# Zero pads and constants filled by VectorE or by ScalarE, and a new order of all operations, in a gated linear attention followed by an MLP mixer

## The chip, the cores and the metric

The kernel runs on one core of a Trainium2 chip. Five engines take part: TensorE (PE; matmuls, with weight loads as a queue of their own), VectorE (DVE), ScalarE (ACT), GpSimd (POOL) and SyncE (SP). Each works through its own list of instructions in order; semaphores tie them together. The metric is the device time of one execution in microseconds (us). Before the change three runs took 174.65, 175.15 and 175.16 us; the median is 175.15.

## The reference

The first half is a gated linear attention over 4 batches, 8 heads, 768 steps and 48 features. Its result, seen as x with 384 features, goes through a mixer: two matmuls over the steps, then two over the features, each pair with a relu between and a residual sum behind.

```python
f = 1.0 / (1.0 + np.exp(-f_logit))
for t in range(S):
    state = f[:, :, t, :, None] * state + np.einsum('bhd,bhe->bhde', k[:, :, t], v[:, :, t])
    y[:, :, t] = np.einsum('bhd,bhde->bhe', q[:, :, t], state)

xt = x.transpose(0, 2, 1)
h = np.maximum(xt @ w_tok1, 0.0) @ w_tok2
u = x + h.transpose(0, 2, 1)
h2 = np.maximum(u @ w_ch1, 0.0) @ w_ch2
return u + h2
```

## The kernel before

Each batch is cut into 6 chunks of 128 steps. For a chunk, ScalarE makes the logarithm of the gate from f (`exp`, then `ln`, lines 366 and 367, or 383 and 387 in batch 0). A low part (`lo`) holds what a bf16 cut of the logarithm leaves out, so that TensorE can add the logarithms up in bf16 with a triangular matrix (`sums`). ScalarE turns the sums into factors `G` and `Gi`, VectorE multiplies q and k by them (`gated`), TensorE transposes both (`turn`), a copy brings them back to SBUF (`turned`), TensorE makes the scores, VectorE masks them (`masked`), and TensorE makes the output of the chunk from the masked scores (`within`, or part of `y`) and from the state of the chunks before (`y`). The state itself goes through `parts` (k times v on TensorE), `tsum` and `state` on VectorE, and `spread`, two copies into a block-diagonal tile `state_bd`. In batch 0 two chunks are handled as a pair (`gates_pair` and `pair`, lines 376 and 590), with other lines for the same steps: sums are L607 and L610, turns L636, parts L657, scores L668, masks L698.

The mixer of a batch follows: `tok1` (L750), a relu into `h1T`, `tok2` (L766), the residual sum `u`, a turn (`ut`, L804, or a transposing DMA), `ch1` (L819) with a relu into `zT` (L352 on ScalarE, L354 on VectorE), `ch2` (L838), the last sum (L844) and the store. The mixer of one batch is interleaved with the attention of the next, so that TensorE has the long matmuls of the one between the short ones of the other.

Nothing of this order is found while the kernel runs. Every operation is recorded in a plan with a number, the engines that may do it and the PSUM bank that it uses. The string `ORDER` (line 34) lists all numbers in the order in which they are issued; a letter behind a number picks the engine (A for ScalarE, D for VectorE, G for POOL, else the first of its list), figures behind colons pick the PSUM banks. An entry `z15` puts 15 filler matmuls of 512 columns (L870) into TensorE's list; they read a tile of ones, `steady`, and write a bank that nobody reads. Since engines work in order, an operation early in the list can hold up everything behind it on its engine.

The loads of q, k, v, of the weights and of f from batch 1 on are issued by POOL (L264 and L270), and their bytes go through one queue. The three loads of f for batch 0 and the stores are issued by SP.

Ahead of all that stand the constants, one operation each (`memset` and `once`, lines 273 to 324): the triangular matrix `tri`, identity and masks, and fills. Heads are 48 wide but laid out in 64 columns, so the columns 48 to 63 of the logarithm `L`, of its low part `Llo` and of the gated `qh` and `kh` are zeroed once; `state_bd` is zeroed, and the last 32 rows of `grow` are filled with ones. All the fills are memsets on VectorE:

```python
    for m in PAIRS:
        memset(f"L{m}p", L[0][:, 2 * m:2 * m + 2, :, D:64], 0.0, [("L", 0, 2 * m), ("L", 0, 2 * m + 1)], 200)
```

## Time and profile before

| | before |
|---|---|
| median of three runs | 175.15 us (174.65 to 175.16) |
| profiled execution | 174.64 us |
| its span, first to last instruction | 172.7 us |
| granted TensorE clock | 1.000 |
| TensorE busy | 164.5 us, 95% |
| VectorE busy | 124.8 us, 72% |
| ScalarE busy | 111.2 us, 64% |
| POOL busy | 81.9 us, 47% |

The profile comes from one execution. Some 1.9 us of it lie outside the span. A share of busy time is a mean over the whole span; TensorE's matmuls overlap and their ends are modelled, so its 95% does not say that it works at its peak. The chain of work that ended last, which is followed back from the last instruction, tells which engine set the end at each moment. In a row of a group stand the line, engine, operation, shapes and count, then the busy time and the mean duration of one in nanoseconds, then the idle time ahead of it and what ended it. A row of the chain or the timeline begins with the start and the duration in microseconds. A row of the stretches gives the limits, the length, then the busy time (and count) of TensorE, its weight loads, VectorE, ScalarE and POOL, the granted clock, the DMA share and GB/s.

### The profile page before, as it was taken

The page shows a single profiled execution, that of the slowest core. Times are in us where ns is not written, and L with a number is a line of the kernel's source. Part 1 is how long each engine was busy: PE and PEld are TensorE (multiplying, and loading weights), DVE is VectorE, ACT ScalarE, POOL GpSimd, SP SyncE. Part 2 cuts the span into 40 slices and gives each one's busy share as a digit, 9 for nine tenths or more (in the row PEclk, how much of TensorE's full clock was granted, in tenths as well). Part 3 has the DMA queues.
Part 4 walks back from the last instruction along what each step waited for, and adds up shares of the span by engine and source line. Part 5 has one row for each costly group of instructions (what it writes and reads, how often), then busy time and mean ns, then how long its engine had stood idle before and what let it go on. Part 6 is the DMA issues. An engine that isn't in the chain of part 4 may idle for free.

```text
span 172.7 us, 4466 instructions
## 1 busy us (share of the span) xinstructions
PE 164.5 (95%) x1764; PEld 103.6 (60%) x1764; DVE 124.8 (72%) x278; ACT 111.2 (64%) x251; POOL 81.9 (47%) x106
## 2 busy tenths in 40 slices
PE   6989899999999999999999999999999999999991
PEld 2457545566676765676667566656665656566660
DVE  5999868798989686989989787777857365433042
ACT  3989596999795637999999755189971410362200
POOL 2999904999636959999759613110001040000000
PEclk9999999999999999999999999999999999999999
DMA  5999999999994899999999954678430036800026
GB/s 149 217 173 181 244 198 209 159 121 111 198 136 26 203 161 127 222 95 91 145 68 112 142 24 91 148 206 197 126 61 6 0 68 211 311 5 0 0 96 229
DMA packets 89573, 22.74 MB, mean 132 GB/s; under 512 B 82288, under 2 KB 88736, under 8 KB 89552
## 3 DMA queue, kind: packets, MB, share of 16 engines
q0 software_dynamic: 69600, 13.77, 93.5%
q1 hardware_dynamic: 19952, 8.69, 19.0%
q8 instruction: 14, 0.23, 0.5%
q14 instruction: 7, 0.06, 0.1%
HBM read 25.17 MB, written 4.72 MB: 173 GB/s over the span
## 4 chain that ended last, share of the span: by engine, by line
PE 78%; ACT 8%; DVE 8%; DMA 2%; issue 2%; DVEq 0%; ACTq 0%
PE ps L819 26%; PE ps L838 24%; PE ps L766 4%; PE ps L750 3%; PE ps L495 3%; PE ps L408 2%; PE ps L560 2%; DMA f_sb<-in_f_logit_dram 2%; DVE AmT L536 2%; PE ps L556 2%; PE ps L870 1%; PE ps L424 1%; PE ps L636 1%; PE ps L456 1%; PE ps L668 1%
## 5 line engine op out<-in xcount | busy, mean ns | idle before, releaser
L819 PE MATMUL ps<-uT,w_ch 128*128 128x384 bf16 x288 | 52.3, 326 | 0.2
L838 PE MATMUL ps<-w_ch,zT 128*128 128x384 bf16 (+2 forms) x300 | 52.4, 320 | 0.0
L352 ACT ACTIVATE zT<-ps 128x384 bf16<-128x384 f32 x64 | 29.5, 490 | 17.3 <-PE ps L819 16.6
L838 PEld LDWEIGHTS <-zT 128*128 128x128 bf16 x300 | 28.0, 98 | 17.2
L819 PEld LDWEIGHTS <-w_ch 128*128 128x128 bf16 x288 | 27.3, 98 | 17.6 <-issue 0.3
L536 DVE TENSOR_TENSOR AmT<-ps,tri_bf 128x512 bf16<-128x512 f32 x36 | 23.4, 684 | 2.0 <-PE ps L408 1.1
L844 DVE TENSOR_TENSOR x_nat<-x_nat,ps 128x384 f32<-128x384 f32 (+2 forms) x25 | 12.8, 534 | 13.2 <-PE ps L838 12.9
L354 DVE TENSOR_SCALAR zT<-ps 128x384 bf16<-128x384 f32 x32 | 16.9, 553 | 7.5 <-PE ps L819 6.7
L348 POOL CAST state_bd<-state 48x192 bf16<-48x192 f32 x19 | 6.5, 342 | 29.8 <-DVE state L549 19.9
L264 POOL DMA_DIRECT2D qk_sb<-in_k_dram x16 | 15.8, 988 | 2.0 <-issue 2.0
L344 ACT ACTIVATE x_bf<-ps 128x384 bf16<-128x384 f32 x17 | 8.4, 492 | 13.0 <-PE ps L560 10.2
L264 POOL DMA_DIRECT2D qk_sb<-in_q_dram x16 | 15.9, 998 | 0.0
L264 POOL DMA_DIRECT2D v_sb<-in_v_dram x16 | 15.8, 989 | 0.0
L348 POOL CAST u_bf<-x_nat 128x384 bf16<-128x384 f32 x12 | 6.6, 564 | 19.2 <-DVE x_nat L782 11.5
L782 DVE TENSOR_TENSOR x_nat<-x_nat,ps 128x384 f32<-128x384 f32 x21 | 10.5, 550 | 4.6 <-PE ps L766 4.6
L750 PE MATMUL ps<-x_bf,w_tok 128*128 128x384 bf16 x48 | 13.3, 326 | 0.1
L374 POOL TENSOR_TENSOR Llo<-L 128x384 bf16<-128x384 f32 x13 | 10.8, 846 | 5.4 <-ACT L L367 5.2
L870 PE MATMUL ps<-x_nat 128*128 128x512 bf16 x32 | 10.8, 471 | 1.5 <-DVE x_nat L279 1.5
L485 DVE TENSOR_TENSOR qk<-qk_sb,GG 128x768 bf16<-128x768 bf16 x18 | 10.1, 569 | 1.0 <-ACT GG L468 0.9
L472 ACT ACTIVATE grow<-ps 32x384 f32<-32x384 f32 x15 | 7.0, 481 | 5.2 <-PE ps L457 5.0
L766 PE MATMUL ps<-h1T,w_tok 128*128 128x384 bf16 x48 | 9.4, 326 | 0.3 <-DVE h1T L354 0.3
L344 ACT ACTIVATE state_bd<-state 48x192 bf16<-48x192 f32 x21 | 7.5, 359 | 3.0 <-DVE state L549 2.3
(96 smaller groups left out, 264.3 us busy)
## 6 DMA issues: line engine op xcount, KB each, us to landing
out_dram<-x_nat SPq DMA_DIRECT2D x23, 192.0 KB, 2.1
f_sb<-in_f_logit_dram POOLq DMA_DIRECT2D x3, 1152.0 KB, 10.8
f_sb<-in_f_logit_dram SPq DMA_DIRECT2D x3, 384.0 KB, 4.1
w_ch<-in_moe_w_ch_dram POOLq DMA_DIRECT2D x2, 576.0 KB, 13.7
qk_sb<-in_q_dram POOLq DMA_DIRECT2D x12, 96.0 KB, 6.5
qk_sb<-in_k_dram POOLq DMA_DIRECT2D x12, 96.0 KB, 6.4
v_sb<-in_v_dram POOLq DMA_DIRECT2D x12, 96.0 KB, 5.0
w_ch<-in_moe_w_ch_dram POOLq DMA_DIRECT2D x1, 1152.0 KB, 10.1
```

The lines of the kernel that those rows point to most:

```text
L264: lambda eng=eng, into=into, of=of: eng.dma_start(out=into, in_=of),
L344: nc.scalar.activation(out_, in_, AF.Copy, bias=0.0, scale=1.0)
L348: nc.gpsimd.tensor_copy(out_, in_)
L352: nc.scalar.activation(out_, in_, AF.Relu, bias=0.0, scale=1.0)
L354: nc.vector.tensor_scalar(out_, in_, 0.0, None, ALU.max)
L536: add(("masked", b, c, p), DVE, lambda half=half, made=made: nc.vector.tensor_tensor(half, made(), tb4, ALU.mult), need=["tri_bf"], make=[ ...
L750: add(("tok1", b, rt, kt), PE, lambda rt=rt, kt=kt, pm=pm: nc.tensor.matmul(banks[pm.at][:, 0:DM], lhsT=w_tok1[:, kt, rt * 128:(rt + 1) * ...
L766: nc.tensor.matmul(banks[pm.at][:, 0:DM], lhsT=w_tok2[:, kt, tt * 128:(tt + 1) * 128], rhs=h1T[:, kt, :], start=(kt == 0 and not held), st ...
L819: nc.tensor.matmul(banks[pm.at][:, 0:384].rearrange("p (n t) -> p n t", t=128), lhsT=w[:, kt, c0:c0 + 128], rhs=uT[:, rows3, kt, :], start ...
L838: nc.tensor.matmul(banks[pm.at][:, 0:n1 - n0], lhsT=zT[:, kt, tt * 128:(tt + 1) * 128], rhs=w_ch2[:, kt, n0:n1], start=(kt == 0), stop=(kt ...
L844: add(("sum", b, tt, n0), DVE, lambda un=un, pm=pm, n=n1 - n0: nc.vector.tensor_tensor(un, un, banks[pm.at][:, 0:n], ALU.add), make=[("x_n ...
L870: nc.tensor.matmul(banks[NBANK - 1][0:rows, 0:cols], lhsT=steady[:, 0:rows], rhs=steady[:, 0:cols], start=True, stop=True)
```

## The change

Three things change. A new helper `fill` records the pads of `L`, `Llo`, `qh` and `kh`, the ones of `grow` and the zeros of `state_bd` as operations that either VectorE (memset) or ScalarE may do; ScalarE writes a copy of `steady`, scaled by the value.

```diff
+    def fill(name, tl, value, make, own, n):
+        op = once(name, (DVE, ACT), None, make, own)
+        def run():
+            if op.engine == DVE:
+                nc.vector.memset(tl, value)
+                return
+            p0 = 128 - tl.shape[0]
+            src, dims = steady[p0:128, 0:n], list(tl.shape[1:])
...
+            nc.scalar.activation(tl, src, AF.Copy, bias=0.0, scale=value)
+        op.fn = run
...
-        memset(f"L{m}p", L[0][:, 2 * m:2 * m + 2, :, D:64], 0.0, [("L", 0, 2 * m), ("L", 0, 2 * m + 1)], 200)
+        fill(f"L{m}p", L[0][:, 2 * m:2 * m + 2, :, D:64], 0.0, [("L", 0, 2 * m), ("L", 0, 2 * m + 1)], 200, 256)
...
-            memset(f"{n}{i}", tl[:, :, D:64], 0.0, [(n, i)], 105)
+            fill(f"{n}{i}", tl[:, :, D:64], 0.0, [(n, i)], 105, 128)
...
-        memset(f"sbd{i}", state_bd[i], 0.0, [("sbd", i)], 200)
+        fill(f"sbd{i}", state_bd[i], 0.0, [("sbd", i)], 140, 384)
```

The string `ORDER` is another one from its first entry to its last. It was made with a longer time set for the fetches of TensorE's instructions. By it, seven fills go to ScalarE. Decoded, the two lists begin so on the engines that the prediction speaks of (`1:` marks a constant, `f`, `q`, `k`, `v` are loads by batch and first chunk, other names are operations by batch and chunk):

```
TensorE before: z15, sums 0, sums 1, sums 2, sums 3, turn 0q, parts 0, turn 1q, turn 0k, turn 2q, turn 1k, sums 5, turn 3q, scores 1, turn 2k, z1, ...
TensorE after:  z14, sums 0, sums 1, z1, sums 2, sums 3, parts 0, turn 0q, turn 0k, turn 1q, turn 1k, sums 4, z2, scores 0, sums 5, turn 2q, scores 1, ...
ScalarE before: exp 0, ln 1, exp 2, ln 0, ln 2, exp 4, ln 4, G 0, Gi 0, G 1, Gi 1, ...
ScalarE after:  1:kh0, 1:L2p, 1:Llo1p, 1:qh1, 1:qh0, 1:L1p, exp 0, ln 0, ln 1, exp 2, ln 2, Gi 0, exp 4, Gi 1, G 1, G 0, ln 4, ...
POOL before:    tri, q0, k0, v0, q2, k2, w_tok1, v2, lo 5, k4, q4, f of batch 1, v4, spread 1, w_tok2, w_ch1, w_ch1, ...
POOL after:     tri, k0, q0, v0, k2, q2, v2, v4, q4, k4, w_tok1, f of batch 1, w_tok2, w_ch1, w_ch1, spread 1, ...
```

From the first loads of chunks 4 and 5 to the second token matmul of batch 0 they go on so:

```
TensorE before: ... within 0, scores 3, y 1, z1, turn 4k, turn 4q, turn 5k, turn 5q, z2, tok1, z1, tok1, tok1, z3, scores 4, tok1, within 2, z3, scores 5, y 2, y 3, z3, parts 4, tok1, within 4, y 4, ...
TensorE after:  ... within 0, z3, scores 3, z2, turn 4k, y 1, turn 5k, turn 4q, z1, turn 5q, scores 2, tok1, z3, scores 5, tok1, z1, scores 4, tok1, tok1, within 2, z3, y 2, parts 4, y 3, within 4, ...
VectorE before: ... gated 4q, gated 4k, gated 5k, gated 5q, state 2, masked 2, masked 3, tsum 3, masked 3, state 3, masked 4, masked 4, masked 5, masked 5, tsum 4, state 4, ...
VectorE after:  ... state 1, gated 4k, gated 4q, gated 5k, tsum 2, masked 3, state 2, gated 5q, tsum 3, masked 3, masked 2, state 3, masked 2, masked 5, masked 4, masked 5, masked 4, tsum 4, state 4, ...
```

The number of filler matmuls is 31 (32 before). Of the operations that may run on more than one engine, 18 relus into `zT` go from ScalarE to VectorE and 14 the other way; seven copies into `u_bf` go from POOL to ScalarE and four back; six low parts go from POOL to VectorE and two back; ten state copies go from POOL to ScalarE and twelve back. The work itself, apart from one filler, is the same.

In the changed file a line ahead of `fill` stands 1 further down and a line behind it 19.

More of the change, by code (lines that the diff above doesn't have):

```diff
@@ L75 @@
[L75 to L77 removed]
+32 33 6D 5D 34 10D 16D 12A 9A 20 15D 8A 13A 0 11A 21 1 7A 35 24 2 27 49 14D 23 36 22 29 26 3 28 50 30 37 51 52D 54 53D
+38 31 25 18D 55 z14 100:0 39 105:1 56D 102 40 58 57D 104 z1 137:2 43 107 106 110 142:3 101 17D 42 59 103 109 41
@@ L78 @@
+1035 1039 1036 1028:2 1046 1047 1040 804 1019 1041 560 1024 1051 1042 1029 1037 1052 1020 1025 1021 1030 1022 1026
+1027 1031 1032
 """
@@ L294 @@
     for m in PAIRS:
-        memset(f"L{m}p", L[0][:, 2 * m:2 * m + 2, :, D:64], 0.0, [("L", 0, 2 * m), ("L", 0, 2 * m + 1)], 200)
-        memset(f"Llo{m}p", Lall[:, 2 * m:2 * m + 2, :, D:64], 0.0, [("Llo", 2 * m), ("Llo", 2 * m + 1)], 110)
+        fill(f"L{m}p", L[0][:, 2 * m:2 * m + 2, :, D:64], 0.0, [("L", 0, 2 * m), ("L", 0, 2 * m + 1)], 200, 256)
+        fill(f"Llo{m}p", Lall[:, 2 * m:2 * m + 2, :, D:64], 0.0, [("Llo", 2 * m), ("Llo", 2 * m + 1)], 110, 256)
     alone = [(b, c) for b, c in sorted(TOTALS) if b or c // 2 not in PAIRS]
@@ L305 @@
     for i in range(NROW):
-        memset(f"grow{i}", grow[i][96:128], 1.0, [("grow", i)], 600)
+        fill(f"grow{i}", grow[i][96:128], 1.0, [("grow", i)], 560, 512)
     for i in range(len(state_bd)):
-        memset(f"sbd{i}", state_bd[i], 0.0, [("sbd", i)], 200)
+        fill(f"sbd{i}", state_bd[i], 0.0, [("sbd", i)], 140, 384)
     if PAIRS:
```

87 lines of the change are left out of this document (44 added, 43 removed).

## The prediction

> **What bounds the kernel now.** I read the shares and the chain of the page first, then the stretches of 8 us, then the chain in order of time.
>
> ```profile
> PE 164.5 (95%) x1764; PEld 103.6 (60%) x1764; DVE 124.8 (72%) x278; ACT 111.2 (64%) x251; POOL 81.9 (47%) x106
> PE 78%; ACT 8%; DVE 8%; DMA 2%; issue 2%; DVEq 0%; ACTq 0%
> ```
>
> TensorE carries the kernel: 78% of the chain. Its busy time is modelled, so what it must do is read from a stretch in which it does nothing else (from the chain in order of time):
>
> ```profile
> 145.52 11.21 PE ps L819 x69
> ```
>
> One matmul of 384 columns takes 11.21/69 = 0.1625 us here, not the 0.32 us of the groups. The change leaves out no real matmul, so only time in which TensorE stands or runs fillers (L870, a 128x512 matmul into an unused bank) can be won. Where is that? The stretches:
>
> ```profile
> 8.00:16.00 8.00, 7.17 (x150) 5.14 (x150) 7.46 (x23) 7.16 (x17) 7.96 (x9) 1.00 1.86 176
> 16.00:24.00 8.00, 6.96 (x150) 4.12 (x150) 6.14 (x15) 6.09 (x12) 5.50 (x8) 1.00 1.36 216
> 24.00:32.00 8.00, 7.45 (x149) 4.43 (x149) 5.96 (x13) 6.38 (x16) 3.70 (x7) 1.00 1.31 203
> 80.00:88.00 8.00, 7.69 (x85) 5.21 (x84) 7.37 (x17) 7.83 (x20) 4.99 (x7) 1.00 2.36 121
> ```
>
> The first figure after the length is TensorE's busy time. Between 8 and 32 us it stands for 0.83 + 1.04 + 0.55 = 2.4 us even by the generous count, and fills more with L870; later a stretch loses 0.31 us at the worst. So the head, up to the first second-stage token matmul (L766), is where a new list can win, and the chain says what it waits for there:
>
> ```profile
> 4.19 0.85 ACT f_sb L387
> 6.76 0.56 DVE Llo L396
> 10.34 0.97 DVE qk L629
> 17.62 0.71 issue
> 21.54 1.03 ACT zT L344
> 22.97 1.03 ACT zT L344
> 24.05 0.42 PE ps L668 x16
> 28.00 0.36 DVE tsum L728
> 28.91 0.36 ACT state_bd L344
> 31.41 1.62 PE ps L766 x9
> ```
>
> From 4 to 12.5 us it is gates: exponential, low part, gated q. One step there is dear, the first gated product at 0.97. From 21.5 to 24 us two copies of transposed q and k stand one after the other on ScalarE before the scores of chunks 4 and 5 (L668). From 28.00 to 31.41 runs a fixed chain (state, its copy, output, x_bf, tok1, relu) of 3.41 us.
>
> **The change, part by part.**
>
> *Fills on ScalarE.* Seven move from VectorE to ScalarE: three strided pads of 128 elements (kh0, qh1, qh0) and three of 256 (L2p, Llo1p, L1p) ahead of the first exponential, and state_bd 1 (384) later, where ScalarE has room. No row of before shows a scaled copy of ones; the nearest are ScalarE's smallest and its usual tile, and on the other side VectorE's zeroing:
>
> ```profile
> L625 ACT ACTIVATE gpair<-ps 128x8 f32<-128x8 f32 x3 | 0.6, 183 | 0.0
> L352 ACT ACTIVATE zT<-ps 128x384 bf16<-128x384 f32 x64 | 29.5, 490 | 17.3 <-PE ps L819 16.6
> L277 DVE MEMSET Llo<- 128x128 uint32 x3 | 0.5, 165 | 0.1
> L277 DVE MEMSET L<- 128x256 f32 x3 | 0.8, 272 | 0.0
> L175 ACT ACT_TABLE_LOAD x1 | 1.3, 1283 | 0.7 <-PEq L888 0.7
> L387 ACT ACTIVATE f_sb<-f_sb 128x768 f32<-128x768 f32 x3 | 2.5, 832 | 2.2 <-DMA f_sb<-in_f_logit_dram 2.2
> ```
>
> On a straight line between 183 (8 elements) and 490 ns (384), 128 elements cost 0.28 and 256 cost 0.39: six fills are 3 x 0.28 + 3 x 0.39 = 2.0 us; the ends are 6 x 0.18 = 1.1 and 6 x 0.49 = 2.9. ScalarE waits 2.17 us for the first f anyway, between its table load (0.74 + 1.28 = 2.02) and the exponential at 4.19. Taken at 2.0 the fills end at 4.0 and cost nothing; at the upper end they end at 4.96 and everything behind the exponential is 0.8 late. I take nothing, by the line. VectorE is relieved of 0.17 + 2 x 0.27 = 0.7 us and three shorter ones, of which only what stands before the low parts counts.
>
> The Trainium skill, "VectorE: DVE Perf Modes", section "Zero memsets can be issued as uint32 (trn2)", speaks against this part: a zero fill of 2-byte elements is done there at 4 bytes per element. The rows agree: Llo's 256 bf16 are 128 uint32 in 165 ns, and ScalarE has no such halving, so the same pad is my 0.39 there. By that rule the change buys some 1 us of VectorE with 2.0 us of ScalarE, a bad trade wherever ScalarE is the later of the two; here the wait for f pays for it.
>
> *First sums.* The list puts logarithm 0 right behind the first exponential and the low parts 0, 1 behind it. VectorE's queue decides: tri at 3.6 us, then ten small constants. Before, eleven such took 3.85 to 5.65, 1.8 us; so the low part of chunk 0 starts near 5.85 (6.76 before), that of chunk 1 ends at 6.95. TensorE's first sums were at 7.12 behind 15 fillers; with 14 they start at 6.9. Gain 0.2.
>
> *No pair of low parts at the same time.* Before, the last one ran on POOL beside VectorE's:
>
> ```profile
> 9.36 1.06 DVE L396 TENSOR_TENSOR Llo<-L 128x384 bf16<-128x384 f32 x1
> 9.97 1.12 POOL L396 TENSOR_TENSOR Llo<-L 128x384 bf16<-128x384 f32 x1
> ```
>
> 1.06 beside POOL, 0.56 alone (6.76 in the chain). The new list has both on VectorE, later, behind the first four gated products: 0.5 us, and the 0.97 product is back at 0.35. What is late next is a load: POOL's queue moves bytes one load behind the other, and its landings are
>
> ```profile
> L264 POOL DMA_DIRECT2D v_sb<-in_v_dram x1: 881/881/881, 5.7 to 5.7; - x1
> DMA to landing us min/median/max: 5.6/5.6/5.6
> L264 POOL DMA_DIRECT2D f_sb<-in_f_logit_dram x1: 2250/2250/2250, 12.8 to 12.8; - x1
> DMA to landing us min/median/max: 11.9/11.9/11.9
> L270 POOL DMA_DIRECT2D w_ch<-in_moe_w_ch_dram x1: 760/760/760, 17.4 to 17.4; - x1
> DMA to landing us min/median/max: 12.6/12.6/12.6
> f_sb<-in_f_logit_dram POOLq DMA_DIRECT2D x3, 1152.0 KB, 10.8
> qk_sb<-in_q_dram POOLq DMA_DIRECT2D x3, 192.0 KB, 5.8
> ```
>
> The first v lands at 5.7 + 5.6 = 11.3, and at 11.4 after, since one more long fill stands ahead of tri. In the new list the parts of pair 0, which need v, stand ahead of its turns, so the turns wait too. Their prices:
>
> ```profile
> 14.68 0.22 PE ps L636 x4
> 14.90 0.35 PE ps L668 x16
> 17.14 0.37 PE ps L657 x32
> ```
>
> Parts from 11.45 to 11.85, four turns to 12.7; the copy of q (ScalarE, 1.03) runs from 12.6 and that of k (VectorE, 0.69) from 12.8, side by side, and the first scores start near 13.8, where before they start at 14.9.
>
> *Chunks 4 and 5.* All nine q, k, v loads of batch 0 now stand ahead of w_tok1. From the first v (11.3) to f of batch 1 (12.8 + 11.9 = 24.7) the queue moved five loads of 192 KB, w_tok1 with 384 and f with 1152: 2496 KB in 13.4 us, 1.03 us for a load. So the last k, six loads behind v, lands at 17.6, and I take 18.6, a load later; w_tok1 two load times on, at 20.6 at the latest. VectorE is through with the masks of pair 0 (four at 0.62 from 14.6, gated products between) at 17.4 and with state 1 at 17.7, so gated products of pair 2 run from 18.7. TensorE: scores 3 to 19.0, two fillers to 19.4, turn 4k, y 1 (its state copy on ScalarE ends at 19.6, behind glast), turn 5k to 20.05; the k copy runs from 20.1 to 21.1. The last q turn waits for gated 5q, which stands behind tsum 2, a mask and state 2 on VectorE and ends at 21.05; the q copy runs from 21.5 to 22.5: scores from 22.55, against 24.05. Five masks then stand on VectorE, at 2.48/4 = 0.62 each:
>
> ```profile
> 15.29 2.48 DVE L698 TENSOR_TENSOR zT<-ps,x_nat 128x512 bf16<-128x512 f32 x4
> ```
>
> Starting at 22.75, behind a state, they end at 25.9, and the chain tsum to L766 of 3.41 us, which is the same operations in both lists, starts at 25.9 instead of 28.0. Gain at this point 2.1 us; the 0.2 of the first sums is in it.
>
> *What I charge against it.* My steps carry no unexplained wait, and before has one, the 0.71 "issue" in the middle of scores at 17.62: TensorE waits for nothing that the profile shows. As many small matmuls stand there in the new list, so I charge 0.7: 1.4 us. The Trainium skill, "Runtime: NRT & Kernel Launch", section "Instruction fetch mechanics", says instructions come in blocks of 256 and that a crossing is mostly hidden; by it I would charge nothing and say 2.1. The trace shows the stall, so the charge stands.
>
> *Behind the head.* Some 95 relus, copies and subtractions change between ScalarE, VectorE and POOL, but the totals hold: 18 relus go to VectorE and 14 come back, and the list has 256 operations for ScalarE (250 before), 276 for VectorE (277) and 97 for POOL (102). What the list does lose is distance: between the turn of chunk 1 of batch 1 and its scores stand one L819 group of three, the parts and one scores, 0.49 + 0.37 + 0.27 = 1.1 us (the small ones from the chain's rows below), where before two groups, a sums and the same parts and scores stood, 1.95.
>
> ```profile
> 44.34 0.36 PE ps L424 x16
> 44.70 0.55 PE ps L408 x16
> L346 DVE COPY qkT<-ps 128x1024 bf16<-128x1024 bf16 x9 | 6.1, 688 | 1.0 <-PE ps L495 1.0
> ```
>
> The copy needs 0.69 and about 0.2 around it, so 0.2 is left instead of 1.0. Going through both lists in this way, I count 12 reads behind the head with under 0.3 us to spare, against 5. One missed costs at most the 0.31 of the worst stretch; I charge two thirds of one, 0.2.
>
> Sum: 2.1 - 0.7 - 0.2 = 1.2 us. The profiled execution took 174.64 with a span of 172.7, so 173.4 and a span near 171.5. The median of the runs, 175.15, lies 0.5 above that execution; from it the sum gives 173.95. I say 173.7, between the two. No change can be told within 0.3%, 0.5 us: 174.6 to 175.7.
>
> **The rivals.**
>
> *Transfers set the head.* TensorE gets ahead, but loads land when they did: f of batch 1 (24.7 before, now with one more load ahead of it, near 25.8) stops ScalarE at its exponential, and behind it in ScalarE's queue stand a state copy and x_bf 5; w_ch1's first half lands at 30.0 whatever the list. For it: POOL's bytes up to there are the same. Against: by my steps L766 starts at 29.3 and the first L819 at 31.5. The state copy is wanted at 25.9 + 0.9 = 26.8 (28.91 - 28.00 in the chain before). If f lands at 27.3 and its exponential takes half a us, the copy is 1.0 late: 173.7 + 1.0 = 174.7.
>
> *Slower: the short distances.* Behind the head the 12 reads with under 0.3 us to spare miss, where ScalarE or VectorE is at 7.4 to 7.9 of 8 (the 80 to 88 stretch). Price up to 0.31 each; seven misses beyond my charge, 2.2 us, turn 1.2 of gain into 1.0 of loss: 173.7 + 2.2 = 175.9. From the third miss on the gain is under 0.5, from the fourth it is a loss. For it: those stretches have no room. Against: L819 groups stand on both sides and give TensorE nothing to lose when a neighbour is early.
>
> *The fills do not hide.* At 0.49 each the first exponential is 0.8 late; the loads hide part of it: 174.5 at the worst.
>
> *All of the 2.1.* No unexplained stall and no miss: 173.7 - 0.9 = 172.8.
>
> **How the numbers follow.** Chances: the sum as worked out 0.44 (173.0 to 174.4); all of the 2.1, 0.14 (172.2 to 173.0); transfers 0.13 (174.7, half of it the same, the rest on either side); fills 0.05 (174.5, mostly the same); short distances 0.24 (175.2 to 177). The range 172.1 to 176.4 leaves out the ends of the first and last. Faster 0.60, the same 0.15, slower 0.25; the likeliest case's own range is 173.0 to 174.4.
>
> **What would show it.** The first L387 at 4.2, no fill behind it; VectorE's Llo at 0.5 each; first L668 near 13.8 in place of 14.9; the first L766 near 29.3 to 30 in place of 31.41; a span of 171.5. I am wrong if TensorE's wait for L387 or for a load shows before 30 us with the first L766 later than 30.9, or if stretches behind 32 us show more than 1 us less busy TensorE than before.

## The result and the profile after

Twenty runs of the changed kernel have a median of 174.44 us, beside 174.95 for the kernel before in runs on the same chip: a ratio of 0.9972, 95% interval 0.9960 to 0.9983, or 0.5 us. The forecast was 1.2 us. The profiled execution took 175.06 us with a span of 173.3, so it lies 0.6 above its median, while the one of before lay 0.3 below its own; what follows therefore compares places in the two traces and not their ends. Of the 0.6 us by which the span is longer, 0.4 lie behind the last sum (4.1 us to the end in place of 3.7).

First the page (shares, then the chain's shares), to be held beside the two lines that open the prediction:

```profile
PE 164.9 (95%) x1758; PEld 103.6 (60%) x1763; DVE 127.8 (74%) x277; ACT 112.2 (65%) x257; POOL 78.0 (45%) x101
PE 77%; ACT 8%; DVE 5%; DMA 4%; issue 3%; POOL 2%; DVEq 0%; ACTq 0%
```

Nothing stands out but that VectorE leaves the chain for the DMA. The chain in order of time says where (start, duration, what):

```profile
3.65 0.29 POOL tri_bf L301
...
5.83 0.86 POOL v_sb L265
6.69 6.26 DMA qk_sb<-in_k_dram
...
23.17 0.42 PE ps L687 x16
24.07 0.35 PE ps L687 x16
30.15 1.46 PE ps L785 x8
...
169.18 0.56 DVE x_nat L863
```

The head now hangs on loads: POOL issues none before the triangle at 3.65, and a load of k issued near 6.7 lands at 12.95. The first second-stage token matmul (L785, L766 before) starts at 30.15 in place of 31.41, 1.26 us earlier. From there to the last sum it takes 169.18 - 30.15 = 139.03 us. The kernel before, by the last row of its chain, took 168.99 - 31.41 = 137.58:

```profile
168.99 0.56 DVE x_nat L844
```

So the tail of the work takes 1.45 us longer. One step of it, `sums` of chunk 0 of batch 1 (two matmuls, 0.33 us), stood ahead of L766 in the old list and stands behind L785 in the new one; the other 1.1 us are lost time. Busy time doesn't show it; the stretch from 32 to 152 us before and after:

```profile
32.00:152.00 120.00, 119.39 (x1189) 76.84 (x1187) 93.09 (x190) 82.51 (x194) 60.09 (x75) 1.00 1.23 126
```
```profile
32.00:152.00 120.00, 119.56 (x1181) 76.37 (x1180) 94.03 (x190) 83.07 (x195) 57.45 (x72) 1.00 1.20 120
```

TensorE is busier after (119.56) with fewer matmul records (1181 against 1189): its matmuls overlap and their ends are modelled, so a group that is held up looks longer. Here are two groups of 16 scores of the changed kernel; inside the second, a matmul waits 0.29 us for a bank:

```profile
44.24 0.62 PE L427 MATMUL ps<-qkT 48*128 48x128 bf16 x16
60.08 0.93 PE L427 MATMUL ps<-qkT 48*128 48x128 bf16 x16
```

So I count from starts: the distance from each matmul to the next, against the usual one (the median for its kind in all traces of this text). Behind the first L766 or L785 the distances add up to 3.0 us over the usual before and 4.1 after. By 70 us the old list has lost 0.5 and the new one 1.8; from there on they lose 2.6 and 2.3. The whole difference is thus made in the first 40 us behind the head. Distances over the usual by more than 0.06 us number 37 before and 46 after. For 29 of them in each kernel (2.9 and 3.0 us) the profile names nothing that was waited for, and all of these stand where one kind of matmul follows another. That leaves 8 named waits before (1.7 us together) and 17 after (2.7). The counts hang on what is taken as usual; the difference, some nine waits and 1.0 us, does so much less.

The weight loads show no more than that. These are the groups of loads from 33.5 us on (busy, mean, idle time ahead), before and then after:

```profile
L819 PEld LDWEIGHTS <-w_ch 128*128 128x128 bf16 x288 | 27.3, 98 | 17.6 <-issue 0.3
L408 PEld LDWEIGHTS <-qkT 48*128 48x128 bf16 x144 | 4.0, 94 | 1.5 <-ACT zT L352 0.3 <-ACT x_nat L344 0.3 <-DVE qkT L346 0.3
```
```profile
L838 PEld LDWEIGHTS <-w_ch 128*128 128x128 bf16 x286 | 27.3, 97 | 17.7 <-issue 0.8
L427 PEld LDWEIGHTS <-qkT 48*128 48x128 bf16 x144 | 4.2, 94 | 2.8 <-issue 1.4 <-ACT qkT L363 0.4 <-DVE qkT L365 0.3
```

The loads of the scores (L408, L427) stand idle for 2.8 us in place of 1.5, but much of that is place and not loss: in both kernels 0.32 to 0.39 us stand ahead of the load in most cases where scores follow a group of 384 columns, four times before and six times after. In the matmul starts only two waits inside groups of scores are new, 0.29 us at 60.41 and 0.20 at 88.27.

### The profile page after: what moved, and what is told of

It is laid out like the page before. It is cut to its first block, busy times and chain, and to the rows that moved or that the text cites. A ratio compares the mean times of both kernels' runs of the same rounds, so it can differ in the third digit from the quotient of the medians.

```text
span 173.3 us, 4461 instructions
## 1 busy us (share of the span) xinstructions
PE 164.9 (95%) x1758; PEld 103.6 (60%) x1763; DVE 127.8 (74%) x277; ACT 112.2 (65%) x257; POOL 78.0 (45%) x101
## 4 chain that ended last, share of the span: by engine, by line
PE 77%; ACT 8%; DVE 5%; DMA 4%; issue 3%; POOL 2%; DVEq 0%; ACTq 0%
PE ps L857 26%; PE ps L838 25%; PE ps L785 5%; PE ps L769 4%; DMA qk_sb<-in_k_dram 4%; PE ps L427 3%; PE ps L514 2%; PE ps L579 2%; PE ps L475 2%; ACT state_bd L363 2%; PE ps L476 2%; ACT zT L371 1%; PE ps L575 1%; PE ps L823 1%; PE ps L443 1%
## 5 line engine op out<-in xcount | busy, mean ns | idle before, releaser
L838 PE MATMUL ps<-uT,w_ch 128*128 128x384 bf16 x288 | 53.3, 326 | 0.3
L371 ACT ACTIVATE zT<-ps 128x384 bf16<-128x384 f32 x60 | 27.5, 498 | 16.8 <-PE ps L838 16.4
L838 PEld LDWEIGHTS <-w_ch 128*128 128x128 bf16 x288 | 27.4, 97 | 18.0 <-issue 1.1
L373 DVE TENSOR_SCALAR zT<-ps 128x384 bf16<-128x384 f32 x36 | 18.8, 550 | 7.3 <-PE ps L838 4.4
L367 POOL CAST state_bd<-state 48x192 bf16<-48x192 f32 x21 | 7.7, 369 | 32.8 <-DVE state L568 19.5
L367 POOL CAST u_bf<-x_nat 128x384 bf16<-128x384 f32 x9 | 4.7, 544 | 24.3 <-DVE x_nat L801 24.3
L487 ACT ACTIVATE GG<-ps 128x384 bf16<-128x384 f32 x18 | 8.9, 499 | 4.7 <-DVE AmT L555 3.0
L504 DVE TENSOR_TENSOR qk<-qk_sb,GG 128x768 bf16<-128x768 bf16 x18 | 11.5, 647 | 0.0
L889 PE MATMUL ps<-x_nat 128*128 128x512 bf16 x26 | 9.4, 488 | 1.9 <-DVE x_nat L298 1.5
L785 PE MATMUL ps<-h1T,w_tok 128*128 128x384 bf16 x48 | 9.9, 326 | 0.6 <-DVE h1T L373 0.6
L393 POOL TENSOR_TENSOR Llo<-L 128x384 bf16<-128x384 f32 x10 | 8.6, 866 | 4.1 <-ACT L L386 4.0
L363 ACT ACTIVATE state_bd<-state 48x192 bf16<-48x192 f32 x19 | 6.8, 359 | 5.7 <-DVE state L568 2.7
## 6 DMA issues: line engine op xcount, KB each, us to landing
f_sb<-in_f_logit_dram POOLq DMA_DIRECT2D x3, 1152.0 KB, 10.8
```

The lines of the kernel that those rows point to most:

```text
L363: nc.scalar.activation(out_, in_, AF.Copy, bias=0.0, scale=1.0)
L367: nc.gpsimd.tensor_copy(out_, in_)
L371: nc.scalar.activation(out_, in_, AF.Relu, bias=0.0, scale=1.0)
L373: nc.vector.tensor_scalar(out_, in_, 0.0, None, ALU.max)
L504: add(("gated", b, c, *names), DVE, lambda n=n: nc.vector.tensor_tensor(qk[it][:, n, :, 0:D], qk_sb[nb][:, n, :, c, :], GG[i][:, n], ALU.m ...
L785: nc.tensor.matmul(banks[pm.at][:, 0:DM], lhsT=w_tok2[:, kt, tt * 128:(tt + 1) * 128], rhs=h1T[:, kt, :], start=(kt == 0 and not held), st ...
```

## The experiments

One table for all kernels, each number from the rows of its own trace: when the first v has landed (issue plus landing), when the parts and the first scores of batch 0 start, when the first second-stage token matmul (`tok2`) starts, and how long it takes from there to the last sum. The median is that of the runs (one time for old_fewer_fillers_first). The two short_relus kernels leave out part of the work.

| kernel | v landed | parts | scores | tok2 | tok2 to last sum | median | ratio to before |
|---|---|---|---|---|---|---|---|
| before | 11.3 | 11.70 | 14.83 | 31.41 | 137.58 | 174.95 | |
| changed | 11.7 | 11.89 | 14.36 | 30.15 | 139.03 | 174.44 | 0.9972 |
| new_head_old_rest | 10.8 | 11.03 | 13.50 | 31.30 | 138.76 | 176.18 | 1.0076 |
| old_head_new_rest | 10.8 | 12.16 | 15.30 | 32.15 | 139.90 | 177.33 | 1.0141 |
| copy_first | 11.0 | 11.15 | 13.62 | 29.41 | 139.01 | 174.58 | 0.9978 |
| fills_on_vector | 11.7 | 11.85 | 14.31 | 29.78 | 139.01 | 174.55 | 0.9981 |
| ones_late | 10.8 | 10.94 | 13.40 | 29.59 | 139.04 | 174.07 | 0.9949 |
| ones_late_copy_first | 11.2 | 11.25 | 13.72 | 29.72 | 139.21 | 174.50 | 0.9977 |
| ones_later | 10.0 | 10.58 | 13.05 | 29.02 | 139.37 | 174.04 | 0.9955 |
| loads_first | 11.1 | 11.72 | 14.65 | 30.24 | 139.38 | 175.08 | 1.0021 |
| old_fewer_fillers_first | 10.8 | 12.16 | 15.30 | 32.05 | 137.59 | 175.22 | |
| other_banks | 11.1 | 11.30 | 13.76 | 29.55 | 140.16 | 175.47 | 1.0029 |
| short_relus_new | 10.7 | 11.02 | 13.48 | 29.40 | 138.04 | 173.17 | 0.9902 |
| short_relus_old | 10.8 | 12.16 | 15.30 | 31.62 | 136.97 | 174.45 | 0.9979 |
| fits | 10.5 | 11.02 | 13.49 | 29.29 | 139.93 | 175.36 | 1.0038 |
| ones_late_fits | 10.6 | 10.68 | 13.15 | 29.73 | 140.03 | 175.37 | 1.0027 |
| ones_late_rotate | 10.6 | 10.86 | 13.33 | 29.34 | 139.00 | 174.12 | 0.9963 |

Two columns carry most of the reading. From parts to tok2 the new list takes 18.25 to 18.27 us in four kernels (changed, copy_first, other_banks, fits) whose parts start anywhere from 11.02 to 11.89: the head moves as a block (18.38 in short_relus_new). And the last stretch takes 139.00 to 139.04 us in five kernels with the new list, and 137.58 and 137.59 in two with the old one: it belongs to the list behind the head, whatever the head did. Only ones_late_copy_first, at 139.21, falls outside with the same list.

The head of the old list is not one number either. The trace that the prediction was made from has the parts at 11.70 and the scores at 14.83; three other traces with the same list up to there have them at 12.16 and 15.30. In these three a small copy on VectorE (64x64, from 9.63) took 1.28 or 1.29 us beside POOL's low part, where the copy of the same shape took 0.20 in the kernel before. So that trace shows an early head: tok2 starts at 31.62 in short_relus_old, whose edit lies behind it.

### Which half of the list

Each half of one list is joined to the other half of the other at the first tok2.

```diff
-ORDER: 32 33 6D ... (new list to the end)
+ORDER: new list up to its first tok2 of batch 0, then what is left in the order of the old list   # new_head_old_rest
+ORDER: old list up to its first tok2 of batch 0, then what is left in the order of the new list   # old_head_new_rest
```

> The new list up to the first second-stage token matmul of batch 0, then everything that is left in the order of the old list. Theory (the gain of the new list lies in its head and is partly given back behind it): the head's gain stays whole, first L785 near 30.1 to 30.2, time about 0.9 below the old kernel's, near 174.0, ratio 0.995. Rival (the head's lead is absorbed, and what gain there is lies in the rest of the new list): no difference to the old kernel, ratio 0.999 to 1.001.

> The old list up to the first second-stage token matmul of batch 0, then everything that is left in the order of the new list. Theory (the rest of the new list costs something, by its shorter distances): first L785 near 31.1, time 0.4 to 1.0 above the old kernel's, 175.3 to 176.0, ratio 1.002 to 1.006. Rival (the gain lies in the rest): about 0.5 below, ratio 0.997.

Both came out slower than either kernel (176.18 and 177.33 us; 1.0050 to 1.0103 and 1.0121 to 1.0161). The seam spoils the sum: in new_head_old_rest the `sums` of batch 1 stand ahead of tok2, as in the old list, and TensorE waits there 1.30 us for ScalarE's logarithm and 0.65 for POOL's low part, so tok2 starts at 31.30 although the scores started at 13.50. For the time as a whole the two kernels settle nothing, and neither forecast was met. Only parts far from the seam can be read: from the `sums` at 42.86 us of the kernel before to the last sum it takes 126.13 us there, and 126.15 behind the new head; from the scores at 60.08 us of the changed kernel it takes 109.11, and 109.09 behind the old head. So what is lost there belongs to the rest of the list and not to how it is reached.

### What sets the head

```diff
 # copy_first: the copy of the turned k of pair 0 ahead of the gated k of pair 1 on VectorE
-... 113A 141 62 116D 144 ...
+... 113A 62 116D 141 144 ...
 # fills_on_vector: the new list with the seven fills back on VectorE, most of them where the old list had them
-... 12A 9A 20 15D 8A 13A 0 11A 21 1 7A ... 19A ...
+... 20 15D 0 21 1 ... 7 9 ... 12 8 13 11 ... 19 ...
```

> The new list with one step moved: VectorE's copy of the transposed k of pair 0 stands ahead of the gated product of chunk 2 that waits for its k load until 13.0. Theory (that load holds up the first scores through VectorE's queue): the first scores L687 start at 13.9 to 14.0 instead of 14.36, and 0.3 to 0.4 of it is left at the first L785 (29.8) and in the time: near 174.1, ratio 0.995. Rival (the load is needed just behind, so the next step is as late as before): first scores earlier, but first L785 within 0.1 of 30.15 and time as the changed kernel's, 174.4, ratio 0.997.

> The new list with its seven ScalarE fills put back on VectorE: L1p and L2p behind exc2, kh0, Llo1p, qh1, qh0 behind the low part of chunk 1, state_bd 1 behind state_bd 0. Theory (moving the fills gives little, since the parts of pair 0 wait for the v load until 11.7 anyway): the first low part starts 0.3 to 0.5 later than 6.61, the first scores within 0.1 of 14.36, time within 0.2 of the changed kernel's 174.4, ratio 0.997. Rival (the fills' 1.0 us on VectorE pass through): first scores 0.5 later or more, time 174.9 to 175.4, ratio 1.000 to 1.003.

copy_first: 174.58 us, 0.9978 (0.9966 to 0.9990), the same as the changed kernel. Its rows on TensorE:

```profile
11.15 0.44 PE L676 MATMUL ps<-v_sb,qk 64*64 64x48 bf16 x32
13.62 0.42 PE L687 MATMUL ps<-zT 48*64 48x128 bf16 x16
```

From parts to scores it takes 2.47 us, as in the changed kernel (14.36 - 11.89), so the order of those two VectorE steps is worth nothing here; the head is only earlier because v landed earlier. fills_on_vector: 174.55 us, 0.9981 (0.9969 to 0.9992): the fills may stand on either engine. Its head is 0.33 us shorter from parts to tok2 (17.93), and the rows of ScalarE show why, first the changed kernel's, then those of fills_on_vector:

```profile
15.49 0.53 ACT L294 ACTIVATE state_bd<-x_nat 128x384 bf16<-128x384 bf16 x1
16.04 0.36 ACT L363 ACTIVATE state_bd<-state 48x192 bf16<-48x192 f32 x1
16.42 0.49 ACT L641 ACTIVATE GG<-ps 128x384 bf16<-128x384 f32 x1
```
```profile
15.57 0.36 ACT L362 ACTIVATE state_bd<-state 48x192 bf16<-48x192 f32 x1
15.96 0.49 ACT L640 ACTIVATE GG<-ps 128x384 bf16<-128x384 f32 x1
```

The seventh fill, the one of `state_bd`, makes a state copy and a factor 0.46 us late. With the fills on VectorE the low part of chunk 0 starts 0.36 later (6.97 against 6.61), which in this execution reaches nothing, since the parts start at 11.85 and 11.89. Why the medians agree in spite of the 0.33 us was not shown.

The next kernels free the first loads. Three fills (the ones of `grow`) that stand ahead of the triangle on VectorE are put later.

```diff
 # ones_late
-... 34 10D 16D 12A 9A 20 15D 8A ... 17D 42 ... 168D 212 ...
+... 34 10D 12A 9A 20 8A ... 42 ... 131 16D 153A ... 168D 15D 17D 212 ...
 # ones_late_copy_first: both edits
 # ones_later: grow 2 behind the last relu of the first h1T turn, grow 0 on ScalarE behind the logarithm of chunk 4 of batch 1
-... 168D 15D 17D 212 ... 223D 228:4 ... 351 250:7 ...
+... 168D 212 ... 223D 17D 228:4 ... 351 15A 250:7 ...
 # loads_first: ones_later with the first k and q issued ahead of the triangle on POOL
-... 21 1 7A 35 24 ... 23 36 22 ...
+... 21 35 36 1 7A 24 ... 23 22 ...
```

> The new list with the three fills of grow with ones (0.48 us each on VectorE, two of them ahead of tri) moved to where VectorE waits anyway: grow1 behind state 1, grow0 and grow2 behind the last x_nat of batch 0 in the head. Theory (the head's chain begins with those fills: they hold up tri, tri the loads of POOL, and the loads the parts and products): first load issued near 2.9 instead of 3.89, first scores 0.5 to 0.9 earlier than 14.36, first L785 0.4 to 0.9 earlier than 30.15, time 173.6 to 174.0, ratio 0.993 to 0.995. Rival (the loads' bytes, not their issue, set the landings, or masks and ScalarE set the head): first load earlier but first scores within 0.2, time as the changed kernel's, 174.4, ratio 0.997.

> Both moves at once: the fills of grow late, and the copy of k ahead of the gated product that waits for its load. Theory (both lie on one chain of loads): the gains overlap, first scores 0.6 to 1.0 earlier than 14.36, time 173.5 to 174.0, ratio 0.993 to 0.995. Rival (neither matters): 174.4 to 174.6, ratio 0.997 to 0.999.

> The changed kernel with its first loads freed of fills as in ones_late, and the two filled copies of ones out of the way of the first h1T turn: the one for the second batch on ScalarE behind the last logarithm of its stretch, the other on VectorE behind h1T(0,1,192). Theory (the head moves as a block with the landing of the v load): the load is issued at 2.4 us, the first scores stand near 13.4 as in ones_late, and the wait ahead of the first tok2 matmul falls back from 1.23 to about 0.8 us, so that tok2 starts near 29.2 and the time is 173.6 to 173.8 us, 0.9 to 1.1 below the kernel before and 0.3 to 0.4 below ones_late. Rival (what the head gains is given back behind it, because the copies there can't follow): tok2 starts earlier, but the last matmul doesn't, and the time stays at 174.1 or more.

> ones_later with the first two loads of k and q issued ahead of the triangle on GpSimd. Theory (the landing of the loads sets the head): the loads are issued some 0.3 us earlier, the parts and the first scores move by 0.2 to 0.3 us, and the time is 173.3 to 173.6 us. Rival (the head is set by VectorE or ScalarE work that doesn't hang on the loads, or the loads land no earlier since they share the DMA engines): the first scores stand where those of ones_later do, within 0.1 us, and the times agree within 0.2 us.

ones_late took 174.07 us, 0.9949 (0.9937 to 0.9962), with ones_later the best of the kernels that do all the work. Its chain and TensorE rows:

```profile
2.47 1.89 POOL qk_sb L264 x2
4.36 0.87 POOL v_sb L264
```
```profile
10.94 0.44 PE L675 MATMUL ps<-v_sb,qk 64*64 64x48 bf16 x32 [0.62 <-DMA v_sb<-in_v_dram]
13.40 0.42 PE L686 MATMUL ps<-zT 48*64 48x128 bf16 x16
29.59 1.46 PE L784 MATMUL ps<-h1T,w_tok 128*128 128x384 bf16 x8 [1.07 <-DVE h1T L372]
```

The v load is issued 1.47 us earlier and lands 0.9 earlier in this pair of traces; the parts wait for it by name. Over all traces it lands at 10.5 to 11.7 us (mean 11.1) in the seven kernels that issue it at 5.8, and at 10.0 to 11.2 (mean 10.6) in the five that issue it at 4.4, so the earlier issue is worth about half a us. Parts and scores come 0.95 earlier, tok2 0.56, since two of the fills now stand on VectorE ahead of the relus that tok2 needs (1.07 of waiting, 0.65 in the changed kernel). ones_later takes that wait back to 0.65 and tok2 to 29.02, yet its time is 174.04 (0.9941 to 0.9969): behind tok2 it takes 139.37 us, 0.33 more, since the fills now stand ahead of the copies for `ut` and `sums` of batch 1. The rival held in the main. With ones_late_copy_first (174.50, 0.9959 to 0.9995) the edits don't add.

loads_first fell outside both theories: 175.08 us, 1.0021 (1.0004 to 1.0039), 1.0 above ones_later. ScalarE's third exponential, ones_later and then loads_first:

```profile
8.05 0.84 ACT L405 ACTIVATE f_sb<-f_sb 128x768 f32<-128x768 f32 x1
```
```profile
9.69 0.84 ACT L405 ACTIVATE f_sb<-f_sb 128x768 f32<-128x768 f32 x1 [1.56 <-DMA f_sb<-in_f_logit_dram]
```

With the loads of k and q issued 1.2 us earlier, the third f of batch 0, which comes through SP's queue, lands at 9.7 in place of 6.8; its exponential starts 1.6 us later, and so do the gates of pair 2. The first v, issued 0.8 earlier, lands at 11.1 in place of 10.0. This is more than chance: that f lands at 6.5 to 6.8 in all eleven kernels whose first load on POOL starts at 3.8 or 3.9, at 6.8 to 8.1 in the five with 2.4, and at 9.7 here with 1.3. So in these traces earlier loads on POOL's queue delay the one on SP's, and issuing still earlier only changes which load is late.

### The unexplained stall

```diff
 # old_fewer_fillers_first: the old list, three fillers moved from the first group to a later one
-... 27 58 z15 ... 47 z3
+... 27 58 z12 ... 47 z6
```

> The old kernel with three of its first 15 fillers moved behind the scores of chunk 2 (12 and 6 instead of 15 and 3). Theory (the 0.71 us in the middle of those scores is a fetch of TensorE's instructions, which comes at a place in its stream): the gap stands three matmuls later in the list, behind the tenth of the 16 matmuls instead of the seventh. Rival (it is a wait on data or a bank): the gap stays behind the seventh, or goes.

TensorE's rows around the stall, before and then with the edit (idle time in brackets):

```profile
17.34 0.28 PE L668 MATMUL ps<-zT 48*64 48x128 bf16 x7
18.33 0.35 PE L668 MATMUL ps<-zT 48*64 48x128 bf16 x9 [0.71 <-issue]
```
```profile
17.81 0.34 PE L668 MATMUL ps<-zT 48*64 48x128 bf16 x10
18.53 0.30 PE L668 MATMUL ps<-zT 48*64 48x128 bf16 x6 [0.39 <-issue]
```

Three instructions less ahead, and the gap moves from behind the 7th matmul of the group to behind the 10th, as forecast. It stands at a place in TensorE's stream of instructions and not at a place in the data, which points to a wait for instructions. The traces do not show that wait itself: the nearest packet of 16 KB in the instruction queue runs from 15.83 to 16.80 us in the kernel before, ahead of the stall. The Trainium skill, "Runtime: NRT & Kernel Launch", section "Instruction fetch mechanics", says that the cost of crossing a 16 KiB boundary is mostly hidden; if this is such a crossing, 0.71 us were not hidden here. The size is not fixed: short_relus_old, with the old list unedited, has 0.46 there and old_head_new_rest 0.73. In the new list the nearest such gap is small, and stands beside a filler:

```profile
18.72 0.59 PE L889 MATMUL ps<-x_nat 128*128 128x512 bf16 x2 [0.16 <-issue]
```

### What is lost behind the head

Seven matmul groups of the changed kernel get other PSUM banks, ones that its trace shows free for longer; nothing else differs.

```diff
 # other_banks
-278:7 282:3 481:1 500:1 552:0 774:6 742:4
+278:2 282:4 481:2 500:5 552:3 774:0 742:3
```

> The new list with nothing moved: seven PSUM banks behind the head are others, so that a matmul group gets a bank that the profile shows free for longer (ch1 of batch 2, groups 0 and 4 of the first and second half; tok2 1 and ut 2 of batch 1; ch1 of batch 0, groups 9 and 11; ch1 10 of batch 1). Theory (the many small waits behind the head are for banks that a relu or copy frees late): the wait of 0.27 ahead of ch1 0 of batch 2 goes, 0.3 to 0.6 in all, time 173.8 to 174.1, ratio 0.994 to 0.995. Rival (the bank is one of several things that end at the same moment, or a neighbour takes the wait over): less than 0.15, time 174.3 to 174.5, ratio 0.997.

175.47 us, 1.0029 (1.0017 to 1.0042), 1.0 us slower than the changed kernel, where a gain of 0.3 to 0.6 was forecast; the stretch behind tok2 takes 140.16 in place of 139.03. Near 120 us TensorE now waits for a relu copy to free a bank:

```profile
120.07 0.65 PE L838 MATMUL ps<-uT,w_ch 128*128 128x384 bf16 x3 [0.29 <-ACT zT L371]
121.19 0.33 PE L475 MATMUL ps<-L,tri_bf 128*128 128x384 bf16 x1 [0.47 <-ACT zT L371]
```

So late banks can cost as much as the whole of the missing time. Do they, in the lists as they are? Of the 17 named waits of the changed kernel, 14 (2.3 us) end when a step of ScalarE or VectorE that reads a PSUM bank, and makes nothing that the waiting matmul reads, is done: it frees the bank. Before, it is 7 of 8 (1.6 us). To test it, the relus behind `ch1` are cut short in both kernels: they write 128 of 384 columns, two groups of the first batch excepted, and leave out the rest.

```diff
 # short_relus_new, short_relus_old
+                wide = 384 if b == 0 and cc >= 10 else 128
+                cols = slice(th * 384, th * 384 + wide)
-                       lambda pm=pm: banks[pm.at][:, 0:384], ...
+                       lambda pm=pm, wide=wide: banks[pm.at][:, 0:wide], ...
```

> The changed kernel in which the rectified copies of the first layer write 128 of their 384 columns, except two groups of the first batch; the rest of the columns keep older values, so that part of the computation is left out. It frees ScalarE and VectorE behind the head and with them the PSUM banks. Theory (the lost TensorE time behind the head comes from banks that the copies free late, and the new list sets more matmuls close behind such copies): from the first tok2 to the last matmul TensorE loses well below 4.2 us, about 2.5, and the difference to the old list with the same edit shrinks from 1.0 us to under 0.4. Rival (the loss lies in the list itself: matmuls that wait for other matmuls' results, instruction fetch, or loads): it stays above 3.5 us, and about 1 us above the old list.

> The kernel before with the same edit: the rectified copies of the first layer write 128 of 384 columns, except two groups of the first batch. Theory (late copies make the waits): TensorE loses about 2.2 us between the first tok2 matmul and the last one, against 3.1 without the edit, and within 0.4 us of the new list with the same edit. Rival (the lists themselves): it loses about 3 us, and the new list with the same edit about 1 us more.

The new list came down by 1.3 us to 173.17 (two runs; 0.9876 to 0.9929 of before), the old one by 0.4 to 174.45 (0.9965 to 0.9993). From tok2 to the last sum it takes 138.04 and 136.97 us, 0.99 and 0.61 less than without the edit; less the 0.33 of the step that changed sides, the new list is 0.74 behind, where it was 1.12. The distances over the usual fall from 4.1 to 3.0 us in the new list (the forecast was a fall from 4.2 to 2.5) and from 3.0 to 2.3 in the old. So shorter relus take a quarter of the lost time away, and a third of the difference; the theory is right in kind and too large in size. The edit also leaves ScalarE and VectorE less to do, so it does not tell a late bank from a late engine. The groups of weight loads, short_relus_new:

```profile
L838 PEld LDWEIGHTS <-w_ch 128*128 128x128 bf16 x283 | 26.9, 98 | 17.0 <-issue 0.2
L427 PEld LDWEIGHTS <-qkT 48*128 48x128 bf16 x144 | 4.2, 94 | 2.8 <-issue 1.6 <-DVE qkT L365 0.3 <-ACT state_bd L363 0.3
```

Those of `ch1` (L838) fall from 17.7 to 17.0; those of the scores stay at 2.8. The two largest waits that are left stand inside groups of scores and end with copies of another kind, which the edit left at full length (x_nat, 0.29 us at 59.14; x_bf, 0.31 at 86.92).

Is it enough, then, to give those matmuls other banks?

```diff
 # fits (changed kernel) and ones_late_fits (ones_late)
-... 742:4 ... 752:1 ...                  # ch1(2,0,0) and ch1(2,0,5)
+... 742:3 ... 752:4 ...
-... 447:0 448:2 454A 455G 451 315 ...    # scores 4, 5 of batch 1; third part of ch2(0,1,0)
+... 315 447:0 448:2 454A 455G 451 ...
-... 396:7 370 365 284:0 ...              # sums(1,2); ch1(0,1,0)
+... 284:0 396:7 370 365 ...
 # ones_late_rotate (ones_late): four banks of one chain
-742:4 752:1 914:3 786:1
+742:3 752:4 914:1 786:3
```

> The changed kernel with three of its waits behind the head taken away by hand, from the releases in its trace: ch1(2,0,0) takes bank 3, free since 115.6 us, in place of bank 4, freed at 119.37 behind G(3,4), and ch1(2,0,5) takes bank 4 in place of bank 1, freed at 120.13 behind zT(2,1,8); the third part of ch2(0,1,0) is put ahead of the scores of chunk 4 of batch 1, which wait for bank 0 until 60.35; ch1(0,1,0), whose bank has long been free, is put ahead of sums(1,2), which waits for bank 7 until 39.24. In the changed kernel these places cost 0.46, 0.25 to 0.33 and 0.23 us. Theory (what the new list loses behind the head are single late banks, each local): TensorE loses about 3.2 us between the first tok2 matmul and the last one, where the changed kernel loses 4.2, and the time falls by 0.8 to 1.0 us to about 173.5. Rival (the copies as a whole can't follow, so a wait taken away stands again at the next tight bank, as with other_banks in the other direction): it loses 3.8 us or more, and the time is that of the changed kernel within 0.4 us.

> The same three edits in ones_late, the fastest kernel so far. Theory (local waits): 173.1 to 173.3 us, 0.8 to 1.0 below ones_late and 1.6 to 1.8 below the kernel before. Rival (the waits stand again at the next tight bank): 173.8 us or more.

> ones_late with one chain of four banks turned round near 119 us: ch1(2,0,0) takes bank 3, ch1(2,0,5) bank 4, sums(3,5) bank 1 and ch1(2,1,10) bank 3, so that, unlike in fits, no later user of a changed bank comes ahead of its release as the trace of ones_late has it. The step costs 0.45 us there. Theory A (the wait is local and gone once the bank fits): TensorE loses 3.7 us from the first tok2 matmul to the last one (4.18 in ones_late), and the time falls by 0.4 to 0.5 us. Theory B (the copies keep the pace, so part of it stands again at the next release): ch1(2,0,2), whose bank 2 VectorE frees at 120.20, then waits some 0.2 us and a later one some 0.1; TensorE loses about 4.0 us, and the time falls by 0.1 to 0.3 us.

fits took 175.36 us, 1.0038 (1.0019 to 1.0057), and ones_late_fits 175.37, 1.0027 (1.0009 to 1.0045). Each of the three waits came back at the next user of a bank, two of them larger:

```profile
61.05 0.81 PE L857 MATMUL ps<-w_ch,zT 128*128 128x384 bf16 x4 [0.63 <-DVE AmT L555]
...
120.71 0.33 PE L475 MATMUL ps<-L,tri_bf 128*128 128x384 bf16 x1 [0.91 <-ACT zT L371]
```

The ch2 group put ahead of the scores had kept them apart from another ch2 that needs their bank; bank 3 was wanted by the sums two steps on. That is partly my own oversight, so ones_late_rotate turns four banks with no such clash. It took 174.12 us, 0.9963 (0.9946 to 0.9981), not to be told from ones_late. TensorE near 119 us in ones_late, then in ones_late_rotate, and VectorE there:

```profile
118.19 2.08 PE L837 MATMUL ps<-uT,w_ch 128*128 128x384 bf16 x9
120.11 0.33 PE L474 MATMUL ps<-L,tri_bf 128*128 128x384 bf16 x1
...
120.93 0.33 PE L574 MATMUL ps<-state_bd,qkT 128*128 128x96 bf16 x4
```
```profile
117.94 1.64 PE L837 MATMUL ps<-uT,w_ch 128*128 128x384 bf16 x9
119.41 0.34 PE L474 MATMUL ps<-L,tri_bf 128*128 128x384 bf16 x1
...
120.00 0.65 PE L837 MATMUL ps<-uT,w_ch 128*128 128x384 bf16 x3
120.59 0.33 PE L574 MATMUL ps<-state_bd,qkT 128*128 128x96 bf16 x4
```
```profile
118.98 0.36 DVE L567 TENSOR_TENSOR state<-tsum,glast 128x192 f32<-128x192 f32 x1 [0.57 <-ACT state_bd L362]
119.26 1.28 DVE L554 TENSOR_TENSOR AmT<-ps,tri_bf 128x512 bf16<-128x512 f32 x2
```

From the first ch1 group (L837) to the sums (L474) it takes 1.47 us in place of 1.92, the 0.45 that the wait had cost. To the outputs (L574) it takes 2.65 in place of 2.74: a few steps on, 0.36 is back, because the next bank is freed by a mask (L554), which stands behind a state update, which waits for ScalarE's state copy. From tok2 to the last sum nothing is left of it (139.00 against 139.04). At this place the pace of the copying engines sets the wait, and a bank only says where it shows. Nor is it the place at which the lists differ: the new one's extra loss is made by 70 us, and of the places that fits changes only those at 39 and 60 us lie there.

What stays open: the 0.7 us of difference that the short relus leave. In these two kernels the waits that end as a bank is freed number 9 (1.3 us) and 5 (0.6), which is of that size, but no run shortened the other copies, so that they cause it was not shown.

## Why the prediction was wrong

**Fills: right in size, wrong for one.** Forecast 0.28 and 0.39 us for 128 and 256 elements and an end at 4.0, hidden by the wait for f. ScalarE's rows:

```profile
2.25 0.40 ACT L294 ACTIVATE L<-x_nat 128x256 f32<-128x256 bf16 x1
2.87 0.49 ACT L294 ACTIVATE qk<-x_nat 128x128 bf16<-128x128 bf16 x2
4.27 0.84 ACT L406 ACTIVATE f_sb<-f_sb 128x768 f32<-128x768 f32 x1 [0.61 <-DMA f_sb<-in_f_logit_dram]
```

A pad of 256 takes 0.40, a small one about 0.3, and after all six ScalarE still waits 0.61 us for f. The seventh, for which I said ScalarE had room, makes a factor 0.46 us late, and the head 0.33 longer than in fills_on_vector. The time is the same with all of them on VectorE, so the part of the change that gives it its name is worth nothing measurable.

**First sums and low parts.** The sums came at 6.82 (6.9 forecast), as the fillers let them. The step behind that was wrong: the low part started at 6.61, not 5.85, because the constants behind the triangle took 2.6 us in place of 1.8. That the sums did not show it is luck, for their first matmul does not read the low part; the second, which does, came at 7.20. The low parts ran at 0.5 us each as forecast (two in 1.03).

**First scores.** Forecast 13.8; they came at 14.36, and at 13.48 to 13.76 in three kernels with the same head (other_banks, fits, short_relus_new). The step was right (the parts wait for v, all turns for the parts), but the landing was taken as one number, 11.4. It is a spread of 10.5 to 11.7 for the same issue time, and moves the head with it.

**Chunks 4 and 5, and the 2.1.** The scores came at 23.17 and 24.07 in place of 22.55, tok2 at 30.15 and, in the kernels with the same head and an earlier v, at 29.29 to 29.55. The forecast for it was 29.3 to 30. So the net gain of the head came out at 1.26 us in this execution and at 1.9 to 2.1 with an early v, where 2.1 - 0.7 = 1.4 was forecast. That 1.4 is near is in part luck: the 0.7 charged for the unexplained stall did not occur (0.16 in the new list), and a late v, by which the parts start 0.4 later than forecast, took its place in this execution. The stall goes with a place in the stream, as old_fewer_fillers_first shows, and was no price to carry over from one list to another. I also left out that the old list does `sums` of the next batch ahead of tok2: 0.33 us of the head's gain is only that step moved behind it.

**Behind the head: the step that failed.** I charged 0.2 us, "two thirds of one" miss at up to 0.31. The runs show 1.1 us, and the stretch repeats to within 0.04 us in five kernels with this list. My count of close reads, 12 against 5, pointed the right way. The price of one miss was not too low: a named wait of the changed kernel takes 0.07 to 0.31 us, 0.16 in the mean. The number of misses was, nine more named waits and not two thirds of one. They were also of another kind: I counted reads of copied data and not the PSUM banks, which make 14 of the 17. I saw no reason for more, because I judged the room by busy time per stretch, which cannot show such waits, as the two rows from 32 to 152 us show. My test for being wrong, more than 1 us less busy TensorE behind 32 us, missed it for the same reason.

**The sum.** Head 1.26 in this execution and up to 2.1 where v lands early, less 1.45 behind it, against the 0.5 us of the medians. The head of the old list also varies, and the trace of before was an early one; against the 31.62 of short_relus_old the head gains 1.5 to 2.3 us. So the medians fit the sum of the two stretches, but no run measured the mean of either head. The rivals: transfers set the head in the sense that the landing of v does, by half a us either way; the one by the f of batch 1 was not seen: it lands at 25.9, as that rival has it, but ScalarE comes to its exponential only at 27.3. "Short distances" names the place and the sign of what took the gain, at half the price that would have made it slower; its mechanism, late reads of copied data, accounts for 3 of the 17 waits.

## What to carry to other kernels

When one list of instructions is exchanged for another, the stage that it was tuned for is only half of the account: measure from one landmark matmul to the last in both traces, for a modelled busy time hides waits of a tenth or two of a us, and there can be many. Count PSUM banks as reads are counted, with the instant at which the last copy frees each one; in four trials here, other banks for a few groups moved the wait or made a larger one. A head that hangs on the first loads gains most by issuing them first (here 0.4 us by moving three fills), until the loads take from one another.

## What the runs showed of the hardware that I had not expected

The landing of one and the same load, 192 KB issued at 5.8 us, took 4.7 to 5.9 us in executions of the same kernel family, more than the whole gain that was measured. Issuing two loads 1.2 us earlier on one queue made a load on another queue land 2.8 us later (9.7 in place of 6.8). TensorE stopped for 0.39 to 0.73 us at a fixed place of its stream in four traces with the old head, and three fewer instructions ahead of it moved the stop by three matmuls; the profile names nothing that it waited for. A copy of 64x64 on VectorE took 1.28 to 1.29 us beside a step of POOL, and 0.20 without it.
